# A fused attention and feed-forward kernel: three evacuations of v moved or reordered, and the later softmax chains rearranged

## Chip, cores and metric

One core of one Trainium2 chip. The metric is the device time of one execution, in microseconds (us), as the median of several executions. Before the change: 508.85 us (three executions, 508.83 to 509.28). A difference of 2% or more (10 us) counts as faster or slower.

Engines are named as the profile names them: PE (TensorE matmul), PEld (its weight loads), DVE (VectorE), ACT (ScalarE), POOL (GpSimd), SP (SyncE, which here only issues transfers).

## The reference

```python
B, N, C = 4, 6208, 256          # q, k, v: float32, [B, N, C]; tau = 1
qn = q / (norm(q, axis=1) + 1e-6);  kn = k / (norm(k, axis=1) + 1e-6)
s = kn.transpose(0, 2, 1) @ qn / tau            # [B, 256, 256]: over the sequence
a = softmax(s)                                  # with + 1e-9 in the divisor
x = v @ a                                       # [B, N, C]
x_prev = x shifted down by one row, zero first
xk = mu_k * x + (1 - mu_k) * x_prev;  xr = mu_r * x + (1 - mu_r) * x_prev
k = relu(xk @ w_k)                              # 256 -> 1024
out = sigmoid(xr @ w_r) * (k * k @ w_v)         # 1024 -> 256
```

## The kernel before

The attention scores need all rows of a batch's q and k, so batch 0 is read first with nothing else to do. After that the kernel walks over 48 blocks of 512 rows of v (12 for each batch), and threads two other things between their matmuls: the squares and products of q and k of the *next* batch ("units"), and, when the units of that batch are done, the "chain" of small pieces that makes its softmax weights `a_sb`. A block's feed-forward part trails its `x = v @ a` by a block or so.

v reaches the kernel by row and is needed by column (`vT`). Blocks 0 to 3 are transposed on PE into PSUM and copied out ("evacuated"); blocks 4 and later are transposed by a transfer that SP issues. In the loads of blocks 0 to 3 a partition holds four neighbouring rows, so that its source is one run of 4 KB; the evacuation then puts the rows in order by reading PSUM with a stride.

```python
    def v_load(i):
        b, t = blocks[i]
        v_bf = p2.tile([P, S, C], BF16, name="v_bf", tag="v_bf", bufs=6)
        nc.gpsimd.dma_start(v_bf, v[b, t * M:(t + 1) * M, :].rearrange(
            "(p s) c -> p s c" if i < S else "(s p) c -> p s c", p=P))
        st[i, "v"] = v_bf

    def v_transpose(i):                         # blocks 4 and later
        v_bf = st.pop((i, "v"))
        vT = p2.tile([P, S, 2, P], BF16, name="vT", tag="vT", bufs=5)
        nc.sync.dma_start_transpose(vT.rearrange("c s h p -> c (s h) p"), v_bf.rearrange("p s c -> p (s c)"))
        st[i, "vT"] = vT

    def v_transpose_pe(i, evac):                # blocks 0 to 3
        v_bf = st.pop((i, "v"))
        vT_ps = ps.tile([P, S, 2, P], BF16, name="vT_ps", tag="kT_ps", bufs=3)
        # ... 8 transposes on PE
        src = vT_ps.rearrange("c s h p -> c h p s")
        if i == 0:
            vT = vT0[:, :, 1:]
        else:
            vT = p2.tile([P, S, 2, P], BF16, name="vT", tag="vT", bufs=5).rearrange("c s h p -> c (s h p)")
            st[i, "vT"] = vT.rearrange("c (h s p) -> c s h p", h=2, s=S)
            vT = vT.rearrange("c (h m) -> c h m", h=2)
        return lambda: evac(vT.rearrange("c h (p s) -> c h p s", s=S), src)
```

The column norms of q and k come from squares that DVE adds up over the row groups (`quad_add`), and from matmuls with ones that add up the partitions (`norms`). The 64 rows left over in each batch are kept apart until then. The chain is a list; one piece is put into the program at each step `j` of a block, and `None` is an empty step. A guard holds the `norms` piece back until the adds have been put into the program, which is when `len(chain) == NORMS`.

```python
        def norms():
            bank[b] = ps.tile([P, 4], F32, name="bank", tag="xT_ps", bufs=2)
            for t, rows in ((sums.pop((b, "left"))[:, 0], L), (sums.pop(b), P)):
                for i in range(4):
                    nc.tensor.matmul(bank[b][:, i:i + 1], t[:rows, i * P:(i + 1) * P], ones[:rows, 0:1], ...)
        # ... roots, pow2, invert, turn, exp (both halves), shares (a power of -1 on GpSimd), weigh (both halves)
        return [evac, None, None, norms, roots, pow2, None, invert, None, None, turn, exp, shares, None, weigh]
    # ...
    AHEAD = 3           # how many groups of the next batch's q and k are fetched ahead of their use
    NORMS = 12
    # ... in the loop over blocks i and steps j:
            if j == 0 and 4 <= i + 6 < NBLK - 1:
                v_load(i + 6)
            if chain:
                piece = chain[0]
                if len(chain) == NORMS and any(e[1] == holds[0] for e in adds):
                    piece = None
                else:
                    chain.pop(0)
                if piece is not None:
                    piece()
            # ... matmuls, squares and mixes of this step
            if (i, j) in ((-1, 6), (0, 4)):
                v_transpose_pe(i + 3, nc.vector.tensor_copy)()      # blocks 2 and 3
            if j == 5 and 4 <= i + 5 < NBLK - 1:
                v_transpose(i + 5)
```

## Time and profile before

| what | before |
|---|---|
| median time | 508.85 us |
| span of the profiled execution | 507.1 us |
| PE busy in the span | 484.2 us (95%) |
| PE waits between 42 and 480 us, by the trace | 1.4 (block 2), 0.3, 0.3, 0.2 us |

The busy table and the waits are quoted in the prediction below. The slices of the page of before: the span cut into 40 equal parts of 12.7 us, each digit the busy share in tenths.

```profile
span 507.1 us, 9288 instructions
...
PEclk9999999999999999999999999999999999999999
DMA  8999999999999999996699999972269664342123
```

The DMA engines are full until slice 18, that is for the first 228 us, and again from 254 to 330 us; the clock row reads 9 throughout. Second, the queue of SP in the time line of before, 74 to 98 us. The columns are start, duration, engine and line, operation, destination and source. The duration is how long the queue is held by *issuing* the transfer; it lands later (median 20.1 us after issue between 60 and 100 us).

```profile
74.59 10.60 SPq L372 DMA_TRANSPOSE vT<-v_bf  x1
85.28 0.53 SPq L560 DMA_DIRECT2D out_dram<-res  x1
85.92 11.95 SPq L372 DMA_TRANSPOSE vT<-v_bf  x1
```

To issue the transpose of one block of v takes 10.6 and 12.0 us here, and PE uses up a block in 10.0 us (its x products of successive blocks start at 82.04, 92.03 and 102.02). SP's queue is never free for more than 0.2 us from 74.59 to 109 us. In this stretch v is delivered more slowly than it is used. Before lives on a reserve: the transposed block 8 lands at 108.8 us and is needed at 112.0, so 3.2 us of it are left. (Landing times of single blocks here and below are the last of the 16 updates of the semaphore that PE waits for, read from the trace file; `prof` has no view of them.)

### The profile page before, as it was taken

What the parts mean: (1) busy time and instruction counts of PE and PEld (TensorE: products, weight loads), DVE (VectorE), ACT (ScalarE), POOL (GpSimd) and SP (SyncE); (2) the same over time, 40 slices, a digit from 0 to 9 for tenths busy, and PEclk for the clock granted to TensorE, in tenths of its full rate; (3) what the DMA queues carried; (4) which work ended last, traced back from release to release, by engine and by line L of the source; (5) the groups of instructions that cost most, each with busy time, mean ns of one, the idle gap of its engine ahead of it and who ended that gap; (6) DMA issues with size and microseconds to landing.
All of it is one profiled execution on the core that took longest, in us unless ns stands there. A gap on an engine that the chain in (4) does not pass through costs nothing.

```text
span 507.1 us, 9288 instructions
## 1 busy us (share of the span) xinstructions
PE 484.2 (95%) x3441; PEld 331.1 (65%) x3441; DVE 431.0 (85%) x784; ACT 428.4 (84%) x868; POOL 98.8 (19%) x146
## 2 busy tenths in 40 slices
PE   3668999999999999999999999999999999999996
PEld 1345667767676676676676776677666666666675
DVE  3778899999989899899889899889978787878884
ACT  5768899989999898888999898988888878888784
POOL 0043242221243323112043322200022100000000
PEclk9999999999999999999999999999999999999999
DMA  8999999999999999996699999972269664342123
GB/s 324 410 320 197 194 172 198 199 163 189 184 192 188 189 188 176 148 201 111 142 146 184 189 185 192 164 152 64 62 146 171 105 144 109 83 92 77 50 76 105
DMA packets 131926, 83.46 MB, mean 165 GB/s; under 512 B 50660, under 2 KB 124712, under 8 KB 131880
## 3 DMA queue, kind: packets, MB, share of 16 engines
q0 software_dynamic: 55056, 33.01, 49.3%
q1 hardware_dynamic: 76504, 49.59, 42.3%
q8 instruction: 27, 0.44, 0.4%
q10 hardware_dynamic: 320, 0.26, 0.2%
q14 instruction: 19, 0.16, 0.1%
HBM read 78.71 MB, written 25.43 MB: 205 GB/s over the span
## 4 chain that ended last, share of the span: by engine, by line
PE 87%; DMA 5%; DVE 4%; ACT 2%; SPq 0%; issue 0%; DVEq 0%
PE vr_ps L545 32%; PE kT_ps L513 31%; PE vr_ps L541 8%; PE xT_ps L405 8%; PE s_ps L262 6%; DMA f<-in_k_dram 5%; DVE kk L526 1%; DVE vT L390 1%; DVE xk L498 1%; ACT xT L407 0%; PE s_ps L190 0%; ACT kr L518 0%; PE y_ps L583 0%; PE x_ps L429 0%; ACT qk L147 0%; PE st_ps L322 0%
## 5 line engine op out<-in xcount | busy, mean ns | idle before, releaser
L518 ACT ACTIVATE kr<-kT_ps 128x512 bf16<-128x512 f32 (+1 forms) x390 | 233.9, 602 | 35.3 <-PE kT_ps L513 31.3
L545 PE MATMUL vr_ps<-w_v_sb,kk 128*128 128x256 bf16 x1536 | 230.3, 273 | 0.0
L513 PE MATMUL kT_ps<-xk,w_k_sb 128*128 128x512 bf16 (+1 forms) x780 | 230.0, 377 | 0.2 <-DVE xk L498 0.2
L545 PEld LDWEIGHTS <-kk 128*128 128x128 bf16 x1536 | 150.3, 98 | 57.3
L526 DVE TENSOR_TENSOR kk<-kr 128x2048 bf16<-128x2048 bf16 (+1 forms) x148 | 125.7, 849 | 1.3 <-ACT kr L518 1.3
L555 DVE SCALAR_TENSOR_TENSOR res<-res,vr_ps 128x256 f32<-128x256 f32 x192 | 79.7, 415 | 52.5 <-ACT res L554 52.5
L513 PEld LDWEIGHTS <-w_k_sb 128*128 128x128 bf16 x780 | 75.5, 98 | 27.5 <-issue 0.6
L554 ACT ACTIVATE res<-vr_ps 128x256 f32<-128x256 f32 x192 | 76.1, 397 | 1.3 <-PE vr_ps L545 1.3
L407 ACT CAST xT<-xT_ps 128x512 bf16<-128x512 f32 x94 | 55.8, 593 | 21.7 <-PE xT_ps L405 21.4
L541 PE MATMUL vr_ps<-w_r_sb,xr 128*128 128x256 bf16 x384 | 73.3, 273 | 0.3 <-DVE res L555 0.3
L498 DVE SCALAR_TENSOR_TENSOR xk<-delta,mu_t,xT 128x512 bf16<-128x512 bf16 x94 | 69.9, 744 | 0.0
L498 DVE SCALAR_TENSOR_TENSOR xr<-delta,mu_t,xT 128x512 bf16<-128x512 bf16 x94 | 69.8, 744 | 0.0
L541 PEld LDWEIGHTS <-xr 128*128 128x128 bf16 x384 | 37.6, 98 | 45.1 <-issue 0.9
L405 PE MATMUL xT_ps<-vT,a_sb 128*128 128x512 bf16 x188 | 55.9, 379 | 1.4 <-DVE vT L390 1.4
L262 PE MATMUL s_ps<-qk 128*128 128x256 bf16 (+1 forms) x294 | 55.8, 273 | 0.0
L127 POOL DMA_DIRECT2D qk<-in_q_dram x39 | 25.9, 665 | 150.6 <-ACT kr L518 123.9
L225 ACT ACTIVATE sq<-qk 128x1024 bf16<-128x1024 bf16 x48 | 50.9, 1061 | 0.0
L364 POOL DMA_DIRECT2D v_bf<-in_v_dram x48 | 36.0, 754 | 42.4 <-DMA vT<-v_bf 30.6
L190 PE MATMUL s_ps<-qk 128*128 128x384 bf16 (+2 forms) x98 | 20.8, 360 | 15.6 <-ACT qk L147 14.5
L488 DVE TENSOR_TENSOR delta<-xT 128x1024 bf16<-128x1024 bf16 x47 | 32.2, 685 | 1.1 <-ACT xT L407 1.1
L262 PEld LDWEIGHTS <-qk 128*128 128x128 bf16 (+1 forms) x294 | 28.5, 98 | 5.6 <-issue 0.8
L190 PEld LDWEIGHTS <-qk 128*128 128x128 bf16 (+1 forms) x98 | 10.1, 105 | 25.9 <-issue 14.8
(105 smaller groups left out, 267.6 us busy)
## 6 DMA issues: line engine op xcount, KB each, us to landing
out_dram<-res SPq DMA_DIRECT2D x47, 512.0 KB, 4.7
v_bf<-in_v_dram POOLq DMA_DIRECT2D x48, 256.0 KB, 8.6
qk<-in_q_dram POOLq DMA_DIRECT2D x36, 256.0 KB, 7.6
qk<-in_k_dram POOLq DMA_DIRECT2D x36, 256.0 KB, 8.8
f<-in_q_dram SPq DMA_DIRECT2D x11, 512.0 KB, 9.5
f<-in_k_dram SPq DMA_DIRECT2D x11, 512.0 KB, 9.9
vT<-v_bf SPq DMA_TRANSPOSE x44, 7.4
f<-in_q_dram SPq DMA_DIRECT2D x2, 256.0 KB, 9.0
```

The source lines that it names most:

```text
L225: nc.scalar.activation(t[:, s:s + 2], qk[:, s:s + 2].rearrange("p s i c -> p s (i c)"), AF.Square)
L262: nc.tensor.matmul(s_ps[:, ih, :], rows_at(qk, b, g, 0)[:rows, s, ih * P:(ih + 1) * P], rows_at(qk, b, g, 1)[:rows, s, :], start=t0 and ih ...
L405: nc.tensor.matmul(xT_ps, a_sb[:, b, ih, dh * P:(dh + 1) * P], vT[:, :, ih, :], start=ih == 0, stop=ih == 1)
L407: nc.scalar.copy(xT[:, dh, 1:], xT_ps)
L498: nc.vector.scalar_tensor_tensor(o[:, dh], st[i, "d"][:, dh], mu[:, dh:dh + 1], st[i, "x"][:, dh, :M], op0=OP.mult, op1=OP.add)
L513: nc.tensor.matmul(kT_ps[:, :m], w_k_sb[:, dh, fh * P:(fh + 1) * P], xk[:, dh, :m], start=dh == 0, stop=dh == 1)
L518: nc.scalar.activation(kr, kT_ps[:, :m], AF.Relu, scale=0.5 ** 0.5)
L526: nc.vector.tensor_tensor(st[i, "kk"][:, fh // 4 * 4 + lo:fh + 1, :m], kr, kr, op=OP.mult)
L541: nc.tensor.matmul(vr_ps[:, D:], xr[:, dh, s * P:(s + 1) * P], w_r_sb[:, dh, :], start=dh == 0, stop=dh == 1)
L545: nc.tensor.matmul(vr_ps[:, :D], kk[:, fh, s * P:(s + 1) * P], w_v_sb[:, fh, :], start=fh == 0, stop=fh == 7)
L554: nc.scalar.activation(res[:, s], vr_ps[:, D:], AF.Tanh, scale=0.5)
L555: nc.vector.scalar_tensor_tensor(res[:, s], res[:, s], 1.0, vr_ps[:, :D], op0=OP.add, op1=OP.mult)
```

## The change

Its intent: take the one large PE wait (1.4 us, block 2) away with ScalarE, make two other evacuations (1.21 us each in before) shorter with plain order, drop twelve small matmuls by adding the left rows in on DVE, and spread or move what the chains put on ScalarE and GpSimd.

```diff
--- before.py
+++ after.py
@@ -58,7 +58,6 @@
     ones = const.tile([P, P], BF16, name="ones")
     ones_f = const.tile([P, 1], F32, name="ones_f")
     half = const.tile([P, 4], F32, name="half")
-    minus = const.tile([P, 4], F32, name="minus")
     vT0 = const.tile([P, 2, M + 1], BF16, name="vT0")
 
     mu_rows = const.tile([4, P], F32, name="mu_rows")
@@ -237,6 +236,8 @@
         if g == 1:
             sums[b] = t[:, 0]
             return
+        if g == 3:
+            nc.vector.tensor_tensor(t[:L, 0], t[:L, 0], sums.pop((b, "left"))[:L, 0], op=OP.add)
         if g == NB:
             to = pq.tile([P, 2 * C], BF16, name="sq", tag="sq", bufs=1)
         elif g == 2:
@@ -273,10 +274,10 @@
         rk = rn[:, 2:4]
         def norms():
             bank[b] = ps.tile([P, 4], F32, name="bank", tag="xT_ps", bufs=2)
-            for t, rows in ((sums.pop((b, "left"))[:, 0], L), (sums.pop(b), P)):
-                for i in range(4):
-                    nc.tensor.matmul(bank[b][:, i:i + 1], t[:rows, i * P:(i + 1) * P], ones[:rows, 0:1],
-                                     start=rows == L and i == 0, stop=rows == P, skip_group_check=True)
+            t = sums.pop(b)
+            for i in range(4):
+                nc.tensor.matmul(bank[b][:, i:i + 1], t[:, i * P:(i + 1) * P], ones[:, 0:1],
+                                 start=i == 0, stop=True, skip_group_check=True)
 
         def roots():
             nc.scalar.copy(rn, bank[b])
@@ -322,8 +323,8 @@
                 nc.tensor.transpose(st_ps[b][:, ih, dh * P:(dh + 1) * P], s_sb[:, dh, ih * P:(ih + 1) * P],
                                     ident_f)
 
-        def exp():
-            for ih in range(2):
+        def exp(halves=range(2)):
+            for ih in halves:
                 if not bounded:
                     nc.vector.tensor_reduce(mx[:, ih:ih + 1], st_ps[b][:, ih], axis=AX, op=OP.max, negate=True)
                     nc.vector.tensor_tensor(mx[:, ih:ih + 1], mx[:, ih:ih + 1], rk[:, ih:ih + 1], op=OP.mult)
@@ -332,11 +333,10 @@
                                      accum_out=sm[:, ih:ih + 1])
 
         def shares():
-            nc.gpsimd.tensor_tensor(sm, sm, minus[:, 0:2], op=OP.pow)
-
-        def weigh():
-            for ih in range(2):
-                nc.scalar.activation(a_sb[:, b, ih, :], e_sb[:, ih], AF.Copy, scale=sm[:, ih:ih + 1])
+            nc.vector.reciprocal(sm, sm)
+
+        def weigh(ih):
+            nc.scalar.activation(a_sb[:, b, ih, :], e_sb[:, ih], AF.Copy, scale=sm[:, ih:ih + 1])
 
         def weigh_first(ih):
             nc.vector.reciprocal(sm[:, ih:ih + 1], sm[:, ih:ih + 1])
@@ -345,9 +345,8 @@
         if b == 0:
             return diagonals, root, invert_first, evac_first, turn, exp, weigh_first
 
-        return [evac, None, None, norms, roots, pow2, None, invert, None, None, turn, exp, shares, None, weigh]
-
-
+        return [evac, None, norms, roots, pow2, None, invert, None, None, turn, lambda: exp([0]), lambda: exp([1]),
+                shares, lambda: weigh(0), lambda: weigh(1)]
 
     blocks = [(b, t) for b in range(B) for t in range(NB)] + ["left"]
     NBLK = len(blocks)
@@ -362,7 +361,7 @@
         b, t = blocks[i]
         v_bf = p2.tile([P, S, C], BF16, name="v_bf", tag="v_bf", bufs=6)
         nc.gpsimd.dma_start(v_bf, v[b, t * M:(t + 1) * M, :].rearrange(
-            "(p s) c -> p s c" if i < S else "(s p) c -> p s c", p=P))
+            "(p s) c -> p s c" if i in (1, 2) else "(s p) c -> p s c", p=P))
         st[i, "v"] = v_bf
 
     def v_transpose(i):
@@ -380,14 +379,16 @@
             for h in range(2):
                 nc.tensor.transpose(vT_ps[:, s, h], v_bf[:, s, h * P:(h + 1) * P], ident)
 
-        src = vT_ps.rearrange("c s h p -> c h p s")
         if i == 0:
-            vT = vT0[:, :, 1:]
-        else:
-            vT = p2.tile([P, S, 2, P], BF16, name="vT", tag="vT", bufs=5).rearrange("c s h p -> c (s h p)")
-            st[i, "vT"] = vT.rearrange("c (h s p) -> c s h p", h=2, s=S)
-            vT = vT.rearrange("c (h m) -> c h m", h=2)
-        return lambda: evac(vT.rearrange("c h (p s) -> c h p s", s=S), src)
+            return lambda: evac(vT0[:, :, 1:].rearrange("c h (s p) -> c s h p", s=S), vT_ps)
+        vT = p2.tile([P, S, 2, P], BF16, name="vT", tag="vT", bufs=5)
+        st[i, "vT"] = vT
+        if i == 3:
+            return lambda: evac(vT, vT_ps)
+        flat = vT.rearrange("c s h p -> c (s h p)")
+        st[i, "vT"] = flat.rearrange("c (h s p) -> c s h p", h=2, s=S)
+        return lambda: evac(flat.rearrange("c (h p s) -> c h p s", h=2, s=S),
+                            vT_ps.rearrange("c s h p -> c h p s"))
 
     def x_half(i, dh):
         b, t = blocks[i]
@@ -594,7 +595,6 @@
     nc.vector.tensor_copy(ident_f, ident)
     nc.vector.memset(ones_f, 1.0)
     nc.vector.memset(half, 0.5)
-    nc.vector.memset(minus, -1.0)
     nc.vector.memset(fill, 1.0)
     nc.vector.memset(vT0[:, :, 0:1], 0.0)
 
@@ -644,7 +644,7 @@
             pos["ld"] += 1
 
     chain = []
-    NORMS = 12
+    NORMS = 13
     holds = [0]
 
     def unit(ahead=2):
@@ -755,7 +755,7 @@
             elif j in (0, 2) and 0 <= i + 1 < NBLK:
                 mix(i + 1, "xr", int(j > 0))
             if (i, j) in ((-1, 6), (0, 4)):
-                v_transpose_pe(i + 3, nc.vector.tensor_copy)()
+                v_transpose_pe(i + 3, nc.vector.tensor_copy if i == 0 else nc.scalar.copy)()
             if j == 5 and 4 <= i + 5 < NBLK - 1:
                 v_transpose(i + 5)
             if i == -1 and j in (5, 6):
```

One `None` ahead of `norms` has gone, so the norms come one step earlier.

## The prediction

> **What bounds the kernel now.** I read the busy table first, then the waits of TensorE (PE) for the whole span and for the stretch after 62 us, and last the timeline of single engines around each place that the change touches.
>
> The busy table:
>
> ```profile
> PE 484.2 (95%) x3441; PEld 331.1 (65%) x3441; DVE 431.0 (85%) x784; ACT 428.4 (84%) x868; POOL 98.8 (19%) x146
> ```
>
> PE is idle for 507.1 - 484.2 = 22.9 us. By stretches, 9.3 us of that lie in the first 20 us and 6.7 in the next 20 (loading q and k of the first batch), 2.5 between 40 and 60, about 0.3 between 60 and 500, and 4.0 at the tail. So from 60 us on the time is the PE's own instruction stream: VectorE (DVE), ScalarE (ACT) or GpSimd (POOL) work saves nothing there unless PE waits for it, and new work there costs nothing until PE does. The PE waits with an end in the changed code, from the waits of the whole span:
>
> ```profile
> PE xT_ps L405 <- DVE vT L390: 1.4, 1, 1.4
> ...
> PE x_ps L429 <- DVE a_sb L343: 0.5, 1, 0.5
> ...
> PE vr_ps L541 <- DVE res L555: 0.3, 1, 0.3
> ```
>
> The largest is one wait of 1.4 us for v of block 2. The PE, ACT and DVE timelines there:
>
> ```profile
> 50.09 0.38 PE L513 MATMUL kT_ps<-xk,w_k_sb 128*128 128x512 bf16 x1 [0.17 <-DVE xk L498]
> 51.83 0.59 PE L405 MATMUL xT_ps<-vT,a_sb 128*128 128x512 bf16 x2 [1.36 <-DVE vT L390]
> ...
> 49.74 0.60 ACT L518 ACTIVATE kr<-kT_ps 128x512 bf16<-128x512 f32 x1 [0.72 <-PE kT_ps L513]
> ...
> 52.46 0.59 ACT L407 CAST xT<-xT_ps 128x512 bf16<-128x512 f32 x1 [1.27 <-PE xT_ps L405]
> ...
> 49.95 0.69 DVE L526 TENSOR_TENSOR kk<-kr 128x1024 bf16<-128x1024 bf16 x1
> 50.56 1.22 DVE L390 COPY vT<-vT_ps 128x1024 bf16<-128x1024 bf16 x1
> ```
>
> The transposes end near 48.84, but DVE reaches the evacuation only at 50.56, after two mixes and a square; ACT meanwhile has holes of 0.72 and 1.27 us.
>
> [...] The old evacuation reads with a stride[...]. [...] the delta subtraction, one of whose inputs starts at an odd element, takes 685 ns for 1024[...]. An odd start of the output, as block 0 will have, no row of this trace shows.
> [...] The one ACT evacuation in the trace, permuted as block 2's will be, took 1005[...].
>
> ```profile
> L390 DVE COPY vT<-vT_ps 128x1024 bf16<-128x1024 bf16 x3 | 3.6, 1213 | 0.0
> ...
> L390 ACT COPY vT<-vT_ps 128x1024 bf16<-128x1024 bf16 x1 | 1.0, 1005 | 0.0
> ```
>
> [...] plain order cuts block 0's and 3's loads into 1 KB source runs in place of 4 KB. [...]
>
> **The change, part by part.**
>
> *Block 2 on ACT.* In ACT's order the copy sits between two activations. It can start at 48.93 (the earlier activation) and, at 1.0 us, ends about 49.93. The next activation moves from 49.74 to about 49.83, the one after stays at 50.5. PE goes on at 50.30 in place of 51.83: the wait of 1.36 goes. ACT is solid from 52.46 to 62, but it too restarts 1.3 us earlier, with the same work behind it. I book **-1.3 us**.
>
> *Block 0 in plain order.* The DVE copy at 38.62 should fall from 1.20 us[...], -0.53. Behind it lie, all on DVE: mu, less, delta, reciprocal, weight (40.53), and PE starts the first products at 40.94. The exponential's sum is there at 39.80, so the reciprocal could go from 40.34 to about 39.87: 0.47 us. Against it: the loads of block 0 and 1 landed 3.9 and 5.4 us after issue (36.6 and 38.75), w_k at 41.7. If each of 512 packets costs the mean of that queue, 49.3% of 16 x 507.1 us over 55056 packets = 73 ns, block 0 takes 32 x 73 ns = 2.3 us of each engine; before, 256 KB at the 190 GB/s of this stretch took about 1.4. So 0.9 us later: block 0 has 0.9 us of slack before its transposes and 0.5 more before DVE would notice, but block 1's transposes and w_k (needed at 42.6, then at 42.15) would come just in time or a little late. I book half, **-0.25 us**.
>
> *Block 3 in plain order.* DVE saves 0.53 at 58.5, where PE doesn't wait: **0**.
>
> *Left row summed in.* Twelve matmuls go, four in each later chain. Eight took 0.29 us to the start of the next matmul (135.04 to 135.33), so four save 0.15: **-0.45 us** for three chains. Three DVE adds of 64x512 (the row of 128x512 bf16 adds says 417 ns) are new and lie in DVE's idle tenth.
>
> *Halves.* Same ACT instructions, spread over two steps. In the third chain both weights ran together at 380.1 to 381.0, held back an ACT tanh, then DVE, and PE waited 0.27 us at 381.34; elsewhere nothing waited. **-0.25 us**.
>
> *Reciprocal on DVE.* 2 elements, about 160 ns (its row for one element: 157) for 707 ns on POOL; nothing waited for POOL's result: **0**.
>
> *Norms one step earlier.* The list loses one empty step ahead of the norms, which now come two steps after the chain starts, at the head of the second half of x's step, not behind it. They need DVE's last add. In chain 1, PE then DVE:
>
> ```profile
> 133.53 0.59 PE L513 MATMUL kT_ps<-xk,w_k_sb 128*128 128x512 bf16 x2
> 133.97 0.71 PE L545 MATMUL vr_ps<-w_v_sb,kk 128*128 128x256 bf16 x5
> 134.51 0.59 PE L405 MATMUL xT_ps<-vT,a_sb 128*128 128x512 bf16 x2
> 135.04 0.43 PE L278 MATMUL bank<-ones,sq 64*128 64x1 bf16 x8
> ...
> 133.94 0.42 DVE L236 TENSOR_TENSOR sq<-sq 128x512 bf16<-128x512 bf16 x1
> 134.40 0.69 DVE L246 TENSOR_TENSOR sq<-acc,sq 128x512 bf16<-128x512 f32 x1
> ```
>
> The add ends at 135.09, just in time for 135.04. One step earlier PE is there at 133.53 and[...] would stand for 135.14 - 133.53 = 1.6 us. The hold in the code looks only at whether the add has been put into the program, which it has (end of the chain's first step), not at whether DVE is that far. In chains 2 and 3 the add comes a step earlier in the program: it ends at 249.25 and 365.31, PE would be there at 249.59 and 365.65, so 0.34 us to spare in both. I book **+1.5 us**. Everything after (roots, inversion, transposes) moves forward with its spacing kept, and the weights end in the same step as before, so block 12, 24 and 36 find them.
>
> Sum: -1.3 - 0.25 - 0.45 - 0.25 + 1.5 = -0.75 us, which is 508.1 us.
>
> **The rivals.** First, no stall of the norms: if DVE ran 1.6 us closer to PE in chain 1 than before, the sum is -2.25, 506.6 us. For it: DVE has less to do early on. Against: DVE is re-timed in each block by a wait for ACT (0.85 us at 126.35, ahead of chain 1), and its work from there to 135.09 is unchanged. Second, the loads hide or eat the start: a 512-packet load of block 0 that lands more than 1.3 us later holds its transposes and everything behind, for a cost of up to 1 us, and block 0's gain turns to a loss: 508.9 to 509.3. For it: the DMA engines are full from 33 to 60 us. Against: the slack above. Third, ACT becomes the bound between 50 and 62 us, where it has no hole: then the 1.3 us would shrink to some 0.3 and the time would be 509. Against: PE waited for no activation in that stretch, and the copy falls into a hole.
>
> **Range and chances.** I am about two thirds sure of the stall. Two thirds of 508.1 and one third of 506.6 give 507.6; with the start a little against me I say **507.8 us**, and **506.3 to 508.9** for 8 in 10: the low end is all gains and no stall, the high end a stall with block 0 spoilt. 2% is 10 us, ten times any term here; I give 0.01 for faster, 0.98 for within 2% and 0.01 for slower.
>
> **What would show each step.** Block 2: the PE wait for L390 gone from the waits and the next products near 50 us; wrong if PE then waits for ACT in 50 to 62. Block 0: its DVE copy near 680 ns and first products near 40.5; [...] if PE waits for v or w_k, the loads did it. Norms: 12 matmuls in place of 24, and in chain 1 a PE wait of about 1.6 us for the last add of sq, none in chains 2 and 3. Halves: no PE wait for res near 380. The prediction is wrong as a whole if PE shows new waits after 62 us other than that one, for DMA above all, since PE then runs nearly 2 us ahead of a full DMA system.

The -0.53 us of the copies of blocks 0 and 3, on which block 0's -0.25 rests, from the rows of before can only be estimated: 1213 ns for the copy with a stride, less 685 ns for the delta subtraction of as many elements, is 0.53 us. That a copy in plain order would be as short as that subtraction, no trace of before shows.

## The result

The four executions of the changed kernel took 506.67, 506.96, 508.10 and 515.58 us: 507.53 us median, beside 509.06 us (508.83 to 509.66) of the kernel before on the same chip. The last is slow. Executions over 1.5% slower than the fastest of the same kernel are left out of the means. The ratio of the fast runs is 0.9962, 95% interval 0.9941 to 0.9984. Such a ratio is the mean time of one kernel's fast runs over that of the other's of the same rounds, so not quite the ratio of the medians. It is 1.9 us of 509, "the same" by the 2% rule. The prediction was 507.8 us, with 506.3 to 508.9 as its range.

The profile of that first measurement fell on the execution of 515.58 us. The changed kernel was therefore run again without an edit, to get a trace of a fast execution (span 505.4 us, the run `after_again` below), and readings of "after" are of that trace unless the slow one is named.

First, the busy table of after:

```profile
PE 478.4 (95%) x3370; PEld 330.4 (65%) x3429; DVE 431.2 (85%) x788; ACT 428.5 (85%) x869; POOL 96.4 (19%) x143
```

3429 weight loads against 3441 before are the twelve matmuls that went. Only 3370 matmuls stand beside them: 59 records are missing from this trace, so the drop in PE's busy time is not a saving. POOL has three instructions less: the powers of -1, now reciprocals on DVE.

Next, the time lines of after around block 2 (PE and ACT), block 0 (DVE and PE) and the norms of chain 1 (DVE and PE):

```profile
49.39 0.38 PE L514 MATMUL kT_ps<-xk,w_k_sb 128*128 128x512 bf16 x1 [0.17 <-DVE xk L499]
49.60 0.59 PE L406 MATMUL xT_ps<-vT,a_sb 128*128 128x512 bf16 x2
...
48.22 1.01 ACT L390 COPY vT<-vT_ps 128x1024 bf16<-128x1024 bf16 x1
...
38.26 0.67 DVE L383 COPY vT<-vT_ps 128x1024 bf16<-128x1024 bf16 x1
...
40.24 0.39 PE L430 MATMUL x_ps<-vT,a_sb 128*128 128x256 bf16 x2 [0.65 <-DVE a_sb L343]
...
131.84 0.42 DVE L235 TENSOR_TENSOR sq<-sq 128x512 bf16<-128x512 bf16 x1
132.29 0.69 DVE L247 TENSOR_TENSOR sq<-acc,sq 128x512 bf16<-128x512 f32 x1
...
133.04 0.25 PE L279 MATMUL bank<-ones,sq 128*128 128x1 bf16 x4 [1.45 <-DVE sq L247]
```

The copy of block 2 takes 1.01 us on ACT, and PE goes straight on at 49.60, where before waited 1.36 us and went on at 51.83. The copy of block 0 has fallen from 1.20 to 0.67 us, and the first products start at 40.24 instead of 40.94. The norms of chain 1, now a step earlier, stand for 1.45 us until DVE's last add ends. That is the stall which was booked.

The waits of PE after 60 us (columns: total, times, longest, in us):

```profile
PE bank L279 <- DVE sq L247: 1.5, 1, 1.5
PE xT_ps L406 <- DMA vT<-v_bf: 0.2, 1, 0.2
```

The second line is new: PE waits for a transposed v. Here it is 0.2 us. In the trace of the slow execution the same list reads:

```profile
PE xT_ps L406 <- DMA vT<-v_bf: 6.2, 2, 3.4
PE bank L279 <- DVE sq L247: 1.4, 1, 1.4
```

To see where the time went, I put one event of each step, the start of the products `xT_ps<-vT,a_sb`, beside the same event of before. A minus is a lead of PE over before, in us. This table is called the ledger below.

| passing | after (fast) | change | after (slow) |
|---|---|---|---|
| block 1, 44 us | -0.71 | start, block 0 | -0.54 |
| block 2, 52 us | -2.23 | -1.52, block 2 | -2.06 |
| block 3, 62 us | -2.45 | -0.22, block 3 | -2.29 |
| block 8, 112 us | -2.11 | +0.34, new DMA wait | +6.24 |
| chain 1, 134.5 us | -0.38 | +1.73, stall | +7.97 |
| after chain 1's old norms, 142 us | -0.77 | -0.39 | +7.58 |
| chain 2, 268 us | -1.07 | -0.30 | |
| end of chain 3, 391 us | -1.59 | -0.52 | |
| last products | -1.59 | | +6.75 |

In the fast trace 2.45 us were won by 62 us, and 2.07 given back by 134.5 us. In the slow one 8.5 us were given back between 92 and 112 us, before the stall was even reached.

Two things help to read the ledger. A wait costs about 0.16 us more than the lists say: of two matmuls of 512 columns the second starts 0.22 us after the first, but each is listed with 0.38 us, and a wait is counted from the end of the last one. So the 1.36 us of block 2 are 1.52 in the ledger, and the 1.45 us of the norms 1.62; the other 0.11 of the +1.73 are the four matmuls that now stand there. And the first row also holds where an execution's start happened to lie: in runs with the old start it reads +0.20 (`b2_only`), +0.01 (`chain_only`) and -0.36 (`before_ahead2`), so the -0.71 is not block 0 alone.

### The profile page after: what moved, and what is told of

The parts are those of the page before. It is cut to its first block, busy times and chain, and to the rows that moved or that the text cites. A ratio compares the mean times of both kernels' runs of the same rounds, so it can differ in the third digit from the quotient of the medians.

```text
span 513.8 us, 9206 instructions
## 1 busy us (share of the span) xinstructions
PE 480.6 (94%) x3370; PEld 330.9 (64%) x3429; DVE 431.4 (84%) x788; ACT 428.6 (83%) x869; POOL 96.4 (19%) x143
## 4 chain that ended last, share of the span: by engine, by line
PE 73%; DMA 21%; DVE 2%; issue 1%; POOL 1%; ACT 1%; SPq 0%; POOLq 0%; DVEq 0%
PE vr_ps L546 28%; PE kT_ps L514 25%; DMA vT<-v_bf 11%; PE vr_ps L542 8%; PE xT_ps L406 7%; DMA f<-in_q_dram 5%; PE s_ps L263 4%; DMA v_bf<-in_v_dram 2%; DMA qk<-in_q_dram 2%; DMA qk<-in_k_dram 1%; POOL v_bf L363 0%; DVE kk L527 0%; SPq L119 0%; PE y_ps L584 0%; PE st_ps L323 0%
## 5 line engine op out<-in xcount | busy, mean ns | idle before, releaser
L514 PE MATMUL kT_ps<-xk,w_k_sb 128*128 128x512 bf16 (+1 forms) x722 | 218.1, 377 | 0.3 <-DVE xk L499 0.2
L189 PE MATMUL s_ps<-qk 128*128 128x384 bf16 (+2 forms) x98 | 19.2, 339 | 17.1 <-ACT qk L146 15.2
L263 PEld LDWEIGHTS <-qk 128*128 128x128 bf16 (+1 forms) x294 | 28.6, 98 | 5.7 <-issue 0.8
L126 POOL DMA_DIRECT2D qk<-in_k_dram x39 | 25.8, 662 | 19.8 <-DMA v_bf<-in_v_dram 11.2
```

The source lines that it names most:

```text
L126: nc.gpsimd.dma_start(rows_at(qk, b, g, i)[:rows, :n], qk_src(t, b, g))
L263: nc.tensor.matmul(s_ps[:, ih, :], rows_at(qk, b, g, 0)[:rows, s, ih * P:(ih + 1) * P], rows_at(qk, b, g, 1)[:rows, s, :], start=t0 and ih ...
L514: nc.tensor.matmul(kT_ps[:, :m], w_k_sb[:, dh, fh * P:(fh + 1) * P], xk[:, dh, :m], start=dh == 0, stop=dh == 1)
```

## The experiments

Twelve runs, each correct, in four calls; all runs of one call share one chip and one set of runs of the kernel before. "Late" executions are those above 514 us (the slowest that is not counted is one of before, 511.72).

| run | median (lowest to highest), us | ratio of fast runs, 95% | late |
|---|---|---|---|
| before | 508.45 (508.12 to 508.93) | | 0 of 11 |
| `after_again` | 511.67 (507.35 to 519.64) | 0.9989, 0.9974 to 1.0003 | 3 of 6 |
| `norms_back` | 507.54 (506.71 to 508.00) | 0.9976, 0.9963 to 0.9989 | 0 of 5 |
| `b2_only` | 507.59 (506.52 to 507.82) | 0.9977, 0.9965 to 0.9989 | 0 of 5 |
| `chain_only` | 509.36 (509.04 to 509.62) | 1.0016, 1.0004 to 1.0028 | 0 of 5 |
| before | 508.86 (508.54 to 510.48) | | 0 of 11 |
| `plain_only` | 508.51 (507.98 to 510.12) | 0.9997, 0.9981 to 1.0013 | 0 of 6 |
| `after_strided` | 508.52 (507.72 to 514.88) | 1.0012, 0.9974 to 1.0049 | 1 of 6 |
| `after_ahead2` | 508.00 (507.18 to 508.92) | 0.9980, 0.9967 to 0.9994 | 0 of 6 |
| `late1_ahead2` | 505.97 (505.26 to 507.45) | 0.9944, 0.9929 to 0.9960 | 0 of 6 |
| before | 509.16 (508.09 to 511.72) | | 0 of 11 |
| `late1` | 507.10 (506.03 to 518.64) | 0.9956, 0.9936 to 0.9976 | 2 of 6 |
| `before_ahead2` | 508.58 (508.54 to 508.71) | 0.9991, 0.9978 to 1.0004 | 0 of 6 |
| `late1_ahead2_b` | 506.08 (505.41 to 507.65) | 0.9944, 0.9927 to 0.9961 | 0 of 6 |
| before | 508.81 (508.25 to 509.68) | | 0 of 9 |
| `block0_strided` | 505.89 (505.79 to 507.65) | 0.9939, 0.9925 to 0.9953 | 0 of 5 |

### The changed kernel once more

No edit; for a fast trace.

> The changed kernel once more, for a profile in the fast state. Theory (parts add up on TensorE): about 1.3 us from block 2, 0.5 from block 0, 0.45 from the twelve matmuls, 0.25 from the halves, less a stall of 1.4 to 1.6 us at the norms of chain 1: span 505.2 to 506.0 against 507.1, and the only new TensorE wait after 62 us is that for sq. Rival (the transfers take it back): even a fast execution shows TensorE waits for the transposed v between 90 and 125 us, as the slow one did (6.2 us), and the stall at the norms is small or gone.

Measured: three of the six executions were late (514.97, 517.23 and 519.64 us), the fast ones took 507.35, 507.99 and 508.37. The fast trace is the one read above. With the first measurement, that is four late executions of ten, and none in the 15 of before that ran beside them. So the late ones belong to the changed kernel and are not only a mood of the chip.

### Norms back in their old place

```diff
-        return [evac, None, norms, roots, pow2, None, invert, None, None, turn, lambda: exp([0]), ...
+        return [evac, None, None, norms, roots, pow2, None, invert, None, turn, lambda: exp([0]), ...
-    NORMS = 13
+    NORMS = 12
```

> The changed kernel with the norms one step later again, as before the change, and one empty step ahead of the transposes dropped so that the weights end in the same step. Theory: the stall of chain 1 goes and nothing takes its place, so 1.4 to 1.5 us faster than the changed kernel in fast runs, near 505.4 us. Rival: TensorE would have waited for a transfer or for another engine soon after in any case, so less than 0.5 us.

The waits of PE after 60 us in this run:

```profile
PE xT_ps L406 <- DMA vT<-v_bf: 1.5, 1, 1.5
PE st_ps L323 <- DVE s_sb L311: 0.5, 1, 0.5
```

The stall has gone, so it was the step that caused it. But the profiled execution kept nothing of it: the wait for the transposed v is 1.5 us in place of 0.2, and the turn, now only one step behind the inversion, waits 0.5 us for DVE. The edit was thus not clean; it moved two things. What it showed is that there is a second limit right beside the first.

### Block 2 alone

```diff
-                v_transpose_pe(i + 3, nc.vector.tensor_copy)()
+                v_transpose_pe(i + 3, nc.vector.tensor_copy if i == 0 else nc.scalar.copy)()
```

> The kernel before with v of block 2 evacuated on ScalarE and nothing else. Theory: 1.3 to 1.5 us faster than before, TensorE's wait of 1.36 us for it gone. Rival (ScalarE has no hole from 52 to 62 us and becomes the bound there): about 0.3 us, with TensorE waits for ScalarE between 50 and 62 us.

Put into before on its own, ScalarE's copy of block 2 took PE from +0.20 to -1.32 in the ledger, -1.52 us, the same as in the whole change. The span was 505.9 us, the ratio 0.9977 (1.2 us). At block 3, 0.15 us were lost again: `res` now waits behind the 1.2 us copy of block 3, by the trace 0.22 us. With a lead of 1.2 us PE waited for no transfer, and no execution was late. But block 8 landed only 0.5 us before its use, where before had 3.2.

### The chain changes alone

Before, with the later half of the diff: left row summed in, halves, reciprocal, norms a step earlier; v as it was.

> The kernel before with the changes of the later chains alone (left row, halves, reciprocal, norms one step earlier), v as before. Theory: 1.45 for the stall less 0.45 less 0.25, so 0.6 to 0.9 us slower than before, near 509.7. Rival (the stall came only with a TensorE that ran ahead, so it does not show here): 0.5 to 0.7 us faster, near 508.3.

The ratio is 1.0016 (1.0004 to 1.0028): taken alone, this half of the change makes the kernel slower, by 0.8 us. The ledger has +1.73 at the stall, then -0.39, -0.29 and -0.52, which leaves +0.53 at the end. Without the 0.11 us of the four matmuls that stay, the stall cost 1.62, so the left row and the halves bring 1.1 us over three chains, and the one step earlier costs more than they bring.

### Plain order alone

Before, with the `v_load` and `v_transpose_pe` of after.

> The kernel before with v of blocks 0 and 3 in plain order and nothing else. Theory (parts add up): the first products 0.5 us earlier, and that kept until 75 us; block 3 gives up to 0.2 us more. In fast runs 0.4 to 0.7 us faster than before. If the small packets of the plain loads are what brings the slow executions (4 of 10 of the changed kernel so far, 0 of 25 without plain order or with less lead), there is one or more among its timed runs; if they come of TensorE's lead on the transfers, none.

The ratio 0.9997 cannot be told from 1. The ledger reads -0.67 at block 1 and -0.90 from block 3 on, to the end. Part of the -0.67 is where that execution's start happened to lie; between 52 and 62 us the plain order of block 3 gave -0.23, where the prediction had 0.

### After with the strided order of blocks 0 and 3

After, with `v_load` and `v_transpose_pe` of before, to ask whether the 1 KB source runs of the plain loads cause the DMA waits.

> The changed kernel with blocks 0 and 3 back in the old order (loads of 4 KB runs, strided evacuation). Theory: 0.5 to 0.7 us of the lead is lost, so TensorE reaches 62 us about 1.75 us before the old kernel, not 2.45; no wait for transposed v above 0.3 us; time within 0.5 us of the changed kernel's fast runs. If the plain loads bring the slow executions: none here. If the lead brings them: fewer than with the full lead, but possible.

They are not what it takes: one execution of six was late (514.88 us), and it is the profiled one, with a PE wait of 3.2 us for a transposed v at 114.63 us. After that wait the clock read 0.50 from 114 to 120 us, which cost another 2.9 us in the ledger. (The fastest of the kernel, 507.72, is only 1.4% below; the interval to 1.0049 is due to that. Without it the five others have a mean of 508.6.)

### Fetching one group less ahead

```diff
-    AHEAD = 3
+    AHEAD = 2
```

> The changed kernel with q and k of the later batches fetched two groups ahead in place of three: the same bytes, asked for later. If the transposes of v are late because the queues are filled too early by q and k, the issue of one transpose between 75 and 100 us takes less than the 12 to 15 us of the changed kernel, TensorE waits for transposed v no more, there is no slow execution, and the fast runs gain 0.3 us. If the transfers are simply too many for this stretch, nothing changes; if the fetch comes too late now, TensorE or ScalarE waits for qk.

The median is 508.00 us, no execution was late, and PE waited for no transposed v; the stall of chain 1 is still there, 1.4 us. In the fast state nothing is gained over after: 508.0 here, 507.2 and 507.9 as means of the fast executions in the two runs of after. They were run at other times.

### Both cures

After with AHEAD = 2, and the norms of chain 1 alone a step later (chains 2 and 3 have their add in time):

```diff
-        return [evac, None, norms, roots, pow2, ...
+        return [evac, None] + [None] * (b == 1) + [
+            norms, roots, pow2, ...
-    AHEAD = 3
+    AHEAD = 2
```

> As the run before, with the norms of chain 1 alone one step later (chains 2 and 3 as in the changed kernel). Theory: the stall of 1.4 to 1.7 us at the norms goes and, if the transfers are relieved, no wait for transposed v takes its place: 1.3 to 1.7 us faster than the run before, near 505.2. Rival (the transfers set the pace of this stretch whatever TensorE does): the gain is taken back by a wait for transposed v, as in the run with the norms back in all chains.

505.97 us, ratio 0.9944 (0.9929 to 0.9960): it beats both kernels, before by 2.8 us. PE shows no wait after 60 us above the trace's threshold. The queue of SP in this run, to be held against the same stretch of before:

```profile
73.89 3.91 SPq L372 DMA_TRANSPOSE vT<-v_bf  x1
83.42 0.38 SPq L562 DMA_DIRECT2D out_dram<-res  x1
83.90 6.60 SPq L372 DMA_TRANSPOSE vT<-v_bf  x1
```

The same transposes hold the queue for 3.9 and 6.6 us in place of 10.6 and 12.0, which is less than PE's 10.0 us for a block; they land 13.5 us after issue (median of 60 to 100 us) in place of 20.1, and the stores of the output 8.1 us after issue in place of 14.6. The edit that matters for this is AHEAD: with q and k of the next batch fetched one group less ahead, v gets through (in `after_ahead2`, too, the same two take 5.3 and 8.4 us, and in `before_ahead2`, which differs from before by this edit alone, 3.9 and 5.9). What it buys is reserve: block 8 lands 9.2 us before its use in `before_ahead2`, against 3.2 in before, and 9.4 us before it in `late1_ahead2`, against 1.4 in `late1`.

### The two cures apart

`late1` has the later norms with AHEAD = 3; `late1_ahead2_b` repeats the version with both; `before_ahead2` gives the kernel before AHEAD = 2.

> The changed kernel with the norms of chain 1 alone one step later, fetch depth 3 as it was. Theory (stall and transfers are two separate losses): no PE wait for the last add of sq in chain 1, and since PE is then still 2.4 us ahead of before from 62 us on, the wait for a transferred vT of 1 to 2 us somewhere in 95 to 120 us (as with the norms put back: 1.5), perhaps a slow execution among the rounds; median 507.0 to 507.6. Rival (the fetch depth does not matter, and late1_ahead2 owes all of its gain to the stall that went): the same 505.9 to 506.2 as with AHEAD 2, and no PE wait for a DMA above 0.3 us.

> The kernel before with AHEAD = 2. Theory (before has 4 us of slack on its transferred v, so a later fetch saves it nothing): same as before within 0.4 us, 508.2 to 509.0, issue of a v transpose on the SP queue between 60 and 100 us down from 8 to 12 us to 4 to 8 us. Rival (a fetch depth of 2 is a gain of its own of over 1 us, for any kernel): 507.5 or less.

> late1_ahead2 once more, beside late1 and before_ahead2 on one chip, so that the three differ by one edit each. Theory: 505.7 to 506.3, ratio 0.993 to 0.996, no slow run, no PE wait for a DMA between 60 and 130 us. Rival (its first result was luck of that chip): 507 or more.

`late1` had two late executions of six (516.53 and 518.64 us); its four fast ones have a mean of 506.6. Its profile has no stall, and, against what I expected, no wait for a transposed v. `late1_ahead2_b` took 506.08 us with no late execution, mean 506.2. The two differ by 0.4 us in the fast state, within their intervals. So in part the rival was right: what the two-cure version gains over after in the *fast* state is the stall; what AHEAD = 2 adds is that no execution was late. And `before_ahead2` is not measurably faster than before (0.9991, 0.9978 to 1.0004), which has 3.2 us of reserve as it is; its executions only lie closer together (508.54 to 508.71, beside 508.09 to 511.72).

One more miss: the profiled execution of `late1_ahead2_b`, the slowest of its six at 507.65 us, does wait for a transposed v:

```profile
PE xT_ps L407 <- DMA vT<-v_bf: 1.7, 1, 1.7
```

It is at 71.73 us, for block 4, the first that is transposed by a transfer. The two transposes issued from 55.69 us on took 9.64 us together. That is another place than the wait of after, and AHEAD = 2 doesn't cure it. Whether it brings it is open: the wait shows in two of the five profiled executions with AHEAD = 2 (the other is `block0_strided`) and in none of the nine with AHEAD = 3.

The profile of `late1` shows one thing about block 0, in PE's time line from 37 us:

```profile
37.38 0.62 PE L381 MATMUL vT_ps<-ident,v_bf 128*128 128x128 bf16 x8
...
39.89 0.62 PE L381 MATMUL vT_ps<-ident,v_bf 128*128 128x128 bf16 x8 [1.14 <-DMA v_bf<-in_v_dram]
40.77 0.38 PE L431 MATMUL x_ps<-vT,a_sb 128*128 128x256 bf16 x2
```

PE waits 1.14 us for the load of block 1, which stands behind the plain load of block 0. From DVE's scaled scores to the first products it is 3.65 us here (37.12 to 40.77), 3.57 in before (37.37 to 40.94) and 3.12 in the trace of after (37.12 to 40.24). The gain of block 0 is lost in this execution. In `late1_ahead2` it is block 0's own load that PE waits for, 0.54 us at 38.01, with a mean clock of 0.55 (38 to 40 us) and 0.60 (40 to 42 us) behind it; there the same stretch took 4.46 us (37.18 to 41.64).

### Block 0 back in the old order

That asks for block 0 alone, in the version with both cures:

```diff
-            "(p s) c -> p s c" if i in (1, 2) else "(s p) c -> p s c", p=P))
+            "(p s) c -> p s c" if i < 3 else "(s p) c -> p s c", p=P))
-            return lambda: evac(vT0[:, :, 1:].rearrange("c h (s p) -> c s h p", s=S), vT_ps)
+            return lambda: evac(vT0[:, :, 1:].rearrange("c h (p s) -> c h p s", s=S),
+                                vT_ps.rearrange("c s h p -> c h p s"))
```

> The version with the norms of chain 1 a step later and AHEAD = 2, with block 0 alone back in the old order (load of 4 KB runs, copy with a stride). Theory (plain order of block 0 saves 0.5 us of DVE time on the path, and loses about as much in executions where the load of 1 KB runs lands late, as in the traces of late1, 1.1 us of PE wait, and of late1_ahead2, 0.5 us and half the clock behind it): the same within 0.5 us, 505.6 to 506.6, PE wait for a loaded v between 36 and 41 us under 0.4 us, copy of block 0 near 1.2 us, DVE's wait-free path from the scaled scores to the first products 3.5 to 3.7 us. Rival A (plain order is a clear gain): 506.6 or more. Rival B (the late load costs more than it brings): 505.5 or less.

505.89 us, ratio 0.9939 (0.9925 to 0.9953): the same as with plain order (0.9944, twice). No wait for a loaded v between 36 and 41 us; the copy took 1.20 us, and the stretch to the first products 3.40 us (37.26 to 40.66), under the 3.5 to 3.7 expected. Four of the five executions lie within 0.15 us (505.79 to 505.94), and the fifth, the profiled one, is at 507.65 with a wait of 1.6 us for block 4's transposed v, as in `late1_ahead2_b`. Plain order for block 0 is worth nothing that can be measured.

## Why the prediction was right, point by point

**The time.** 507.8 was predicted, 507.53 measured; the means of the fast executions are 507.2 and 507.9, and the sum without hedging, 508.1, is a little above both. That the number fits so well is in part luck. Block 2, block 3 and the left row brought more than was booked, block 0 and a new wait for transfers less, and these misses cancelled. And only one of the first four executions was late: of the six of `after_again` three were, and their median, 511.67, lies outside the range. The class was sure from the start.

**What bounds the kernel: right.** PE sets the pace from 60 us to the end; a lead in the ledger, once won, stays to the last row unless PE has to wait again.

**Block 2, -1.3: right, -1.52 in three traces.** The difference is the 0.16 us by which a wait costs more than it reads. The wait went whole, and ScalarE didn't become the bound, as the third rival had it: PE shows no wait for ACT in 50 to 62 us.

**Block 0, -0.25: the two halves were right, no net can be told from zero.** The copy fell from 1.20 to 0.67 us, although its output starts at an odd element (block 3's plain copy, with an even start, took 0.685), and the stretch by 0.45 us in the trace of after, against 0.47 worked out. The loads that come late, booked as half of that, made PE wait for 0 to 1.1 us by execution (0.8 in `after_ahead2`, 1.1 in `late1`; in the old order 0 to 0.4), so the second rival was partly right. Over executions nothing that can be measured is left, as `block0_strided` shows.

**Block 3, 0: wrong by a little, -0.22.** "PE doesn't wait" was read from a list that leaves out short waits. In `b2_only`, with the lead won and the copy still 1.2 us, `res` shows the wait, 0.22 us.

**Norms one step earlier, +1.5: right.** The wait read 1.45 us and cost 1.62, where 1.6 was worked out from the trace's end of the add; none in chains 2 and 3. The first rival, no stall, falls.

**Left row, -0.45: mis-sized, about -0.85. Halves, -0.25: right.** In chain 2, where nothing else changed, the gain is 0.30 us in place of 0.15: four matmuls hold PE for 0.10 us (248.43 to 248.53 in `late1_ahead2`), eight for 0.29 (251.10 to 251.39 in before). I had taken half of the eight. That is 0.19; the other 0.10 lies ahead of the eight, since the two x products before them take 0.53 us to the next start (250.57 to 251.10) in place of the usual 0.43. Why they do is open. Chain 1 brings as much (0.39 less the 0.11 of the matmuls that stay). Chain 3 lost its wait for `res` besides (0.27 us in before, none in after), and its 0.52 less 0.28 is the 0.24 that was booked.

**The missing term: transfers after 62 us.** The prediction named it as what would make it wrong as a whole ("PE shows new waits after 62 us other than that one, for DMA above all") but gave it no number. It came, so by its own test the account was incomplete although the time was met: 0.3 us in a fast trace, 1.5 in `norms_back`, and most of 8.5 in the slow one. How the lead meets the transfers can be seen in SP's queue in the fast trace of after:

```profile
72.66 12.15 SPq L371 DMA_TRANSPOSE vT<-v_bf  x1
84.90 0.53 SPq L561 DMA_DIRECT2D out_dram<-res  x1
85.53 12.01 SPq L371 DMA_TRANSPOSE vT<-v_bf  x1
```

PE is 2.45 us ahead, so everything is asked for earlier, but the second transpose starts only 0.39 us earlier than in before (85.53 for 85.92), since the first holds the queue for 12.15 us instead of 10.60. The reserve at block 8 is eaten from both sides: it lands at 109.87, 1.06 us later than in before, and is asked for 2.45 us earlier. That is 0.3 us more than the 3.2 there were, and PE waits. So the better PE did early, the sooner it ran into this: a part of the expected gain, 0.3 us in this trace, was turned into a new wait.

**The late executions.** Their trace in the first measurement, PE waits first and then two stretches with the columns us, busy time of PE, PEld, DVE, ACT and POOL, clock, DMA share and GB/s:

```profile
103.00 1.01 PE L406 MATMUL xT_ps<-vT,a_sb 128*128 128x512 bf16 x2 [2.71 <-DMA vT<-v_bf]
...
118.26 0.59 PE L406 MATMUL xT_ps<-vT,a_sb 128*128 128x512 bf16 x2 [3.44 <-DMA vT<-v_bf]
```

```profile
75.00:80.00 5.00, 5.00 (x40) 3.62 (x38) 4.97 (x10) 4.42 (x10) 0.54 (x1) 1.00 1.91 43
...
103.00:106.00 3.00, 3.00 (x11) 1.53 (x11) 1.05 (x3) 1.95 (x4) 0.75 (x1) 0.50 1.34 233
```

Between 75 and 80 us the share of the DMA engines reads 1.91 (by single us 6.97, 0.54, 0.33, 0.07 and 1.64; in before 1.35 over the five), and yet they move 43 GB/s, where before moved 164. The transposes in SP's queue then take 13.2 and 15.2 us, PE waits at 103.00, and comes back to half the clock for some 3 us: 11 matmuls in place of 24. So the slowness starts with the transfers, and the lower clock comes after the wait; in the ledger it costs 1.5 of the 8.5 us. Not every wait is followed by it: after the one of 3.44 us in the same trace the clock read 1.00 (110 to 130 us), while in `late1_ahead2` a mean of 0.55 to 0.60 came after one of 0.54 us. What decides it, no run shows.

Such a jam takes neither the changed kernel nor a late execution. In `before_ahead2` the transfers move 25 GB/s from 90 to 94 us, and PE, with 9.2 us of reserve at block 8, doesn't stop (columns as above; the second number is PE's busy time):

```profile
90.00:94.00 4.00, 4.00 (x31) 2.82 (x30) 3.97 (x9) 3.13 (x8) 1.81 (x3) 1.00 0.72 25
```

And the late execution of `after_strided` has no such jam (156 GB/s from 75 to 80 us); its transposes hold the queue for 12.4 and 12.6 us all the same.

What is shown: late executions were 7 of 27 in the changed kernel and its variants with AHEAD = 3 (`after` and `after_again` 4 of 10, `late1` 2 of 6, `after_strided` 1 of 6, `norms_back` 0 of 5), 0 of 23 in its variants with AHEAD = 2, and 0 of 68 in before, `b2_only`, `chain_only`, `plain_only` and `before_ahead2` (46, 5, 5, 6 and 6). The runs were made on several chips; on the two where the changed kernel's variants ran at both depths it is 3 of 12 with AHEAD = 3 against 0 of 18 with 2, a split that chance alone would give about once in 18. What is only argued: that it is the earlier requests which tip a full DMA system over. The jam in `before_ahead2`, whose PE is only 0.36 us ahead of before, speaks against it, and for the plainer reading that delays come anyway and a kernel with little reserve can't ride them out; that isn't shown either. Why so little is moved in a jam, and why only in some executions, no run settles. `after_strided` shows that the plain loads of blocks 0 and 3 are not needed for a late execution.

## What to carry to other kernels

Where an engine sets the pace and its supply has little reserve, first measure that reserve (when each piece lands against when it is needed, and the time the issuing queue needs for one against the time of one block); time won early comes out of it: here a lead of 2.45 us, with a landing 1.06 us later, turned 3.2 us of reserve into a wait of 0.3. A guard on "already put into the program" is no guard on "already done": moving a consumer one step up can make its engine stand until the producer is done, as PE did for 1.45 us at the norms of chain 1. And when something is fetched far ahead while the transfers are full, try one less: here it cost nothing that could be measured, and none of 23 executions was late with it.
